# A long-convolution and rational-feed-forward kernel: narrower tiles, and a filter network fed by feature

## The chip, the cores and the metric

The kernel runs on one core of a Trainium2 chip. It has five engines with instruction queues of their own: TensorE (PE in the profile, with its weight loads as PEld), VectorE (DVE), ScalarE (ACT), GpSimd (POOL) and SyncE (SP), which here only issues transfers. The metric is device time of one execution in microseconds. The kernel before takes 2253.34 us, the median of three runs (2252.31 to 2254.02).

## The reference

```python
def _attn_ref(x, v, pos_emb, w1, w2):            # B, S, D = 2, 12480, 128; pos_emb is S x 64
    h_mlp = np.maximum(pos_emb @ w1, 0.0) @ w2
    h_filt = h_mlp * np.exp(-0.01 * np.arange(S))[:, None]
    Uf = np.fft.rfft(x * v, n=2 * S, axis=1)
    Hf = np.fft.rfft(h_filt, n=2 * S, axis=0)
    y = np.fft.irfft(Uf * Hf[None], n=2 * S, axis=1)[:, :S]
    return x * y

def _moe_ref(x, w_in, w_out, a, b):              # x: 24960 x 128, w_in: 128 x 2048
    h = x @ w_in
    P = a[0] + a[1] * h + a[2] * h**2 + a[3] * h**3
    Q = 1.0 + np.abs(b[0]) * np.abs(h) + np.abs(b[1]) * h**2
    return (P / (Q + 1e-06)) @ w_out
```

The result of the first function, seen as 24960 rows, is the input of the second. A long filter is made by a small network from `pos_emb` (the filter network), weighted by a decaying window, and convolved with x·v through a Fourier transform. Then comes a feed-forward layer with a quotient of two polynomials as its nonlinearity.

## The kernel before

**Positions.** A position is written as n = m·128 + residue (`N2` = 128, `H2` = 64). There are 12480 = 97·128 + 64 positions, so a residue below 64 has 98 of them (`M` = 98 rows m) and a residue from 64 up has 97. Of the window only the first 82 rows are used (`MF`).

**Stage one** (batch 0 and the filter) begins with the filter network in 16 blocks of `NP` = 4 pairs of residues, one from the upper half and its mirror from the lower half. `load_pos` fetches `pos_emb` for a block with four transfers on SP's queue, rows m on the partitions (L276). `hf_w` multiplies it by the window with two VectorE instructions of 82 x 256 elements (L480, L486), one block ahead. `hf_t` turns the four pairs by four transposes on TensorE (L500) and copies the result on ScalarE (L503), so that the two times 64 features lie on the partitions. `hf_1` is the product with w1 and the relu (L507, L509), `hf_2` the eight passes of the product with w2 (L515) and four copies (L521). Blocks are pipelined: iteration i runs `hf_t(i)`, `hf_1(i - 1)`, `hf_2(i - 2)`.

Into the same iterations other work is laid. From iteration 5 on each one advances `weights_gen`, which turns a tile of 256 columns of w_in from 64-bit to 32-bit numbers with integer work on VectorE (L330 to L339, L346) and two steps on GpSimd (L341, L455); step k runs in iteration k + 5 and issues the load of tile k + 2 (`raw`, L317). In iterations 0 to 7 a part of x·v is multiplied on GpSimd (L245), and the next parts of x and v are loaded (`xq`, `vq`, L237 and L238). All these loads stand in SP's queue in the order of the code. Each engine takes its instructions in order.

Behind the blocks 32 channel groups go through the transforms. The first of VectorE's work there is L563 (`tb`, 128 x 720), which multiplies by twiddle factors.

**Stage two** is the feed-forward layer: 52 tiles of five residues (or four, at the end of a half), 26 per batch, each in four steps of four blocks of 128 of the 2048 features, 208 steps. All tiles have 98 positions per residue, 490 columns (392 for four residues), whether the last position exists or not. Tiles with p0 below 64 (numbers 0 to 12 and 26 to 38) hold the residues from 64 up. A step computes h with three products (L870 to L872), abs of h (`q`: L880 on halves, or L887 and L893), square of h (`v`, L904), L914 on VectorE, the square of q (L932, L937 on ScalarE, or L942 and L943 on GpSimd for one of the four rows), ln (L948), exp (L953), L959 and L964 on VectorE, L969 and L975 on GpSimd and the product with w_out (L987). A half is two rows of a tile's width (2 x 490 = 980 elements per partition), a whole four. The order in which the steps are issued comes from two strings, `FIRST` for steps 0 to 94 and `REST` for the others; they differ in which engine gets which part of a step. Beside the steps, batch 1's transforms and the next tile's input (`attn_a`, `attn_b`) are laid into slots. `store` copies a finished tile (L998, L1001) and writes it with transfers on SP's queue (L1009). Since the rows of the output are 128 positions apart and pieces may not cross 128 partitions, a tile takes seven or eight of these.

Of the kernel before, what the change touches and what calls it, by code (L numbers as in the profile page):

```python
# [9 lines left out]
F32 = mybir.dt.float32  # L10
# [8 lines left out]
FO = 64  # L19
DFF = 2048  # L20
N2 = 128
M = 98
# [39 lines left out]


def constants():
    t = np.arange(N2)
# [29 lines left out]
    win[:S] = WINDOW  # L95
    win = win.reshape(M, N2)[:96]
    return {
# [12 lines left out]
@with_exitstack  # L110
def build(ctx: ExitStack, tc, x, x_q, v_q, pos_emb, w1, w2, w_in, w_out, moe_a, moe_b,
          f1_d, tw_d, twh_d, dft_d, dfth_d, idfth_d, g_d, win_d, ident_d, out):
# [144 lines left out]
    with ExitStack() as st:  # L257
# [3 lines left out]
        flat = [sp.tile([128, CG * 2 * K1], F32, tag=t, name=t + "0", bufs=2) for t in ("ta", "ta", "tb")]  # L261
        win, bdw1, bdw2 = flat[0][0:96, 0:N2], flat[1][:, 0:128], flat[2][:, 0:2 * D]
        twh = sp.tile([N2, 2, 2 * K1], F32, name="twh")
# [3 lines left out]

        NPL = 4
        pos_t = {}

        def load_pos(p0):
            t = sp.tile([M, 2 * NPL, FO], F32, tag="wa", name="pos", bufs=3)
            for o, t0 in ((0, H2 + p0), (NPL, H2 - p0 - NPL)):
                if MF < M:
                    for r0, r1 in ((0, MF // 16 * 16), (MF // 16 * 16, MF)):
                        nc.sync.dma_start(out=t[r0:r1, o:o + NPL], in_=rows(pos_emb, r0, r1 - r0, t0, NPL, 0, FO))  # L276
                else:
                    load_rows(t[:, o:o + NPL], pos_emb, t0, NPL, 0, FO, True)
            pos_t[p0] = t
# [192 lines left out]

        nb = H2 // NP
        W = NP * MF
        pT, rT = {}, {}

        def hf_w(p0):
            t = pos_t[p0]
            pw = pos_t[p0] = sp.tile([MF, NPL, 2, FO], F32, tag="wb", name="pw", bufs=2)
            nc.vector.tensor_tensor(out=pw[:, :, 0], in0=t[0:MF, 0:NPL],  # L480
                                    in1=win[0:MF, H2 + p0:H2 + p0 + NPL].unsqueeze(2).to_broadcast([MF, NPL, FO]), op=ALU.mult)

            a, w = t[0:MF, 2 * NPL - 1], win[0:MF, H2 - 1 - p0:H2 - p0]
            a = bass.AP(a.tensor, a.offset, [list(a.ap[0]), [-FO, NPL], [1, FO]])
            w = bass.AP(w.tensor, w.offset, [list(w.ap[0]), [-1, NPL], [0, FO]])
            nc.vector.tensor_tensor(out=pw[:, :, 1], in0=a, in1=w, op=ALU.mult)  # L486

        def hf_t(i):
            p0 = i * NP
            b0 = p0 // NPL * NPL  # L490
            if p0 == b0:
                if b0 + 3 * NPL < H2:
                    load_pos(b0 + 3 * NPL)
                if b0 + NPL < H2:
                    hf_w(b0 + NPL)
            pt = pos_t[b0]
            ps = cvs()
# [24 lines left out]

        hf_w(0)
        load_pos(2 * NPL)
        sg = scalars()
# [120 lines left out]
    def second_part(short):  # L646
# [138 lines left out]
        def residue(p0, n):  # L785


            return H2 + p0 if p0 < H2 else N2 - p0 - n

        def load_xg(j):  # L790
            if j >= len(tiles):
                return
            b, p0, n = tiles[j]
            xt = mp.tile([M, NPT, D], F32, tag="xt", name="xt", bufs=2)
            load_rows(xt[:, 0:n], xb[b], residue(p0, n), n, 0, D, True)
            gt = mp.tile([K1, NPT, 2, M], F32, tag="gt", name="gt", bufs=2)
            nc.sync.dma_start(out=gt[:, 0:n], in_=g_d[:, p0:p0 + n])
            xg[j] = (xt, gt)
# [28 lines left out]
        def attn_b(j):  # L827
            n = tiles[j][2]
            w = n * M
            take_up()  # L830
            t = an.pop(j)

            def fill(cv):
                for i in range(n):
                    nc.tensor.transpose(out=cv[:, 0, i * M:(i + 1) * M], in_=t[:, i, :], identity=ident[0:M, 0:M])
# [17 lines left out]
        def width(s):  # L853
            return tiles[steps[s][0]][2] * M

# [134 lines left out]
        def store(j):  # L990
            b, p0, n = tiles[j]
            n0 = residue(p0, n)
            w = n * M
            t = mp.tile([128, 4, D], F32, tag="ot", name="ot", bufs=2)
            a = acc.pop(j)
            nq = (w + 127) // 128
            full = w // 128
            nc.vector.tensor_copy(out=t[:, 0:full, :], in_=a[:, 0:full, :])  # L998
            if full < nq:
                k = w - full * 128  # L1000
                nc.vector.tensor_copy(out=t[0:k, full, :], in_=a[0:k, full, :])  # L1001
            ob = out[b * S:(b + 1) * S, :]
# [73 lines left out]


def by_quarter(x):
# [3 lines left out]
    return a.transpose(0, 4, 2, 1, 5, 3)  # L1082


# [21 lines left out]
```

## Time and profile before

| | us |
|---|---|
| median of three runs | 2253.34 |
| the profiled execution | 2255.12 |
| its span | 2253.2 |
| TensorE busy | 2023.2 (90%) |
| VectorE busy | 2073.7 (92%) |
| ScalarE busy | 1941.2 (86%) |
| GpSimd busy | 2021.5 (90%) |

The span is what the profiler's records cover. The busy shares are means over stages that differ: in the first fortieths of the span ScalarE and GpSimd are about half busy, and the transfers are densest there; in the second half all four engines are over 80%. So what a single stage waits for is read from a view of that stage (busy times by stretch, the timeline, the chain of waits), and the groups by shape give the duration of one instruction. In a timeline row the two numbers are the start and the duration; a bracket tells when the instruction's input was ready and what released it.

### The profile page before, as it was taken

Reading aid. Unit: us, or ns where it says so; the run is one execution under the profiler, and the core shown is the slowest. Engines: PE = TensorE matmul, PEld = TensorE weight load, DVE = VectorE, ACT = ScalarE, POOL = GpSimd, SP = SyncE. Lnnn points to the kernel's source line nnn. Section 1 sums busy time; section 2 is a strip of 40 time slices with the busy share of each in tenths; the row PEclk is TensorE's granted clock in tenths of the full one; section 3 lists DMA queues with packets and bytes.
Section 4 is the critical chain, followed back from the end, with each engine's and each line's share of the span. In section 5 each row is a group of like instructions: output and inputs, shape, how many; then the busy total and the mean of one; then the engine's idle time right before and its main releaser. Section 6 shows DMA issues by size and latency. Waiting matters only on the chain.

```text
span 2253.2 us, 35705 instructions
## 1 busy us (share of the span) xinstructions
PE 2023.2 (90%) x13344; PEld 1758.5 (78%) x13344; DVE 2073.7 (92%) x2374; ACT 1941.2 (86%) x1971; POOL 2021.5 (90%) x1605
## 2 busy tenths in 40 slices
PE   6899987899999999999999889888888898888887
PEld 4678775788888888888888777777777777777775
DVE  6899995899998998999999789999999999999996
ACT  5422224999999998999999899999999999999996
POOL 5488765999999999999999789999999999999997
PEclk9999998999999999999999999999999999999999
DMA  5344415433143233223222212212112111221100
GB/s 159 107 142 143 130 62 146 106 94 81 36 117 80 51 87 83 70 60 76 58 62 52 49 33 46 48 34 46 31 36 49 38 40 33 48 48 33 36 10 11
DMA packets 169487, 150.31 MB, mean 67 GB/s; under 512 B 91622, under 2 KB 138984, under 8 KB 166424
## 3 DMA queue, kind: packets, MB, share of 16 engines
q1 hardware_dynamic: 162280, 124.17, 22.5%
q10 hardware_dynamic: 7024, 23.76, 3.2%
q8 instruction: 107, 1.75, 0.3%
q14 instruction: 76, 0.62, 0.1%
HBM read 99.72 MB, written 48.17 MB: 66 GB/s over the span
## 4 chain that ended last, share of the span: by engine, by line
ACT 41%; POOL 22%; PE 22%; DVE 7%; issue 5%; DMA 2%; SPq 1%; POOLq 0%; DVEq 0%; ACTq 0%
POOL v L975 10%; ACT v L904 10%; ACT l L948 9%; ACT r L953 9%; PE acc L987 5%; POOL v L969 4%; ACT q L880 4%; ACT q L937 4%; ACT q L932 3%; PE cs L155 3%; PE cs L582 2%; POOL q L943 2%; PE cv L816 2%; PE h L870 1%; PE h L872 1%
## 5 line engine op out<-in xcount | busy, mean ns | idle before, releaser
L975 POOL TENSOR_TENSOR v<-v,q 128x980 f32<-128x980 f32 (+1 forms) x416 | 940.6, 2262 | 52.0 <-DVE q L964 48.7
L987 PE MATMUL acc<-wout,v 128*128 128x128 f32 (+2 forms) x6656 | 846.2, 280 | 112.4 <-POOL v L975 108.0
L987 PEld LDWEIGHTS acc<-wout,v 128*128 128x128 f32 (+2 forms) x6656 | 776.6, 187 | 191.5 <-POOL v L975 165.8
L959 DVE SCALAR_TENSOR_TENSOR q<-q,sc,r 128x980 f32<-128x980 f32 (+1 forms) x416 | 504.6, 1213 | 36.3 <-ACT r L953 34.9
L914 DVE SCALAR_TENSOR_TENSOR v<-v,sc,h 128x980 f32<-128x980 f32 (+1 forms) x416 | 504.7, 1213 | 35.4 <-ACT q L880 30.4
L964 DVE SCALAR_TENSOR_TENSOR q<-q,r 128x980 f32<-128x980 f32 (+1 forms) x416 | 482.0, 1159 | 13.5
L904 ACT ACTIVATE v<-h,sc 128x980 f32<-128x980 f32 (+1 forms) x416 | 438.1, 1082 | 30.9 <-PE h L872 29.4
L953 ACT ACTIVATE r<-l 128x980 f32<-128x980 f32 (+1 forms) x416 | 416.8, 1002 | 9.8 <-DVE q L964 8.9
L969 POOL TENSOR_SCALAR v<-v,sc 128x980 f32<-128x980 f32 (+3 forms) x321 | 422.3, 1316 | 0.0
L948 ACT ACTIVATE l<-q,sc 128x1960 f32<-128x1960 f32 (+1 forms) x208 | 401.1, 1928 | 0.7 <-POOL q L943 0.5
L870 PE MATMUL h<-ahi,win_l 128*128 128x490 f32 (+1 forms) x832 | 360.9, 434 | 28.6 <-DVE v L914 26.6
L871 PE MATMUL h<-alo,win_h 128*128 128x490 f32 (+1 forms) x832 | 319.6, 384 | 0.0
L872 PE MATMUL h<-ahi,win_h 128*128 128x490 f32 (+1 forms) x832 | 317.6, 382 | 0.0
L880 ACT ACTIVATE q<-h 128x980 f32<-128x980 f32 (+1 forms) x303 | 302.5, 998 | 8.9 <-PE h L872 8.8
L870 PEld LDWEIGHTS h<-ahi,win_l 128*128 128x128 f32 x832 | 158.6, 191 | 60.5 <-DVE v L914 38.4
L932 ACT ACTIVATE q<-q,sc 128x1960 f32<-128x1960 f32 (+1 forms) x95 | 185.9, 1957 | 0.0
L872 PEld LDWEIGHTS h<-ahi,win_h 128*128 128x128 f32 x832 | 158.0, 190 | 26.0
L937 ACT ACTIVATE q<-q,sc 128x1470 f32<-128x1470 f32 (+1 forms) x113 | 170.6, 1510 | 0.0
L871 PEld LDWEIGHTS h<-alo,win_h 128*128 128x128 f32 x832 | 159.2, 191 | 13.5 <-DVE alo L841 0.4
L816 PE MATMUL cv<-yc,gt 90*98 90x128 f32 x1004 | 127.9, 274 | 2.2 <-DVE an L822 1.0
L816 PEld LDWEIGHTS cv<-yc,gt 90*98 90x98 f32 x1004 | 118.3, 165 | 14.1 <-DVE an L822 7.5
L943 POOL TENSOR_TENSOR q<-q 128x490 f32<-128x490 f32 (+1 forms) x113 | 111.4, 986 | 9.4
(113 smaller groups left out, 2623.5 us busy)
## 6 DMA issues: line engine op xcount, KB each, us to landing
yc<-y_d SPq DMA_DIRECT2D x23, 900.0 KB
gt<-in_g_dram SPq DMA_DIRECT2D x48, 344.5 KB
xq<-in_x_q_dram SPq DMA_DIRECT2D x64, 196.0 KB
vq<-in_v_q_dram SPq DMA_DIRECT2D x64, 196.0 KB
h_d<-hg ACTq DMA_DIRECT2D x32, 360.0 KB
y_d<-ys ACTq DMA_DIRECT2D x16, 720.0 KB
hg<-h_d SPq DMA_DIRECT2D x64, 180.0 KB
y_d<-ys SPq DMA_DIRECT2D x16, 720.0 KB
```

The lines of the kernel that those rows point to most:

```text
L870: nc.tensor.matmul(out=t[:, k, 0:w], lhsT=wl, rhs=hi[:, 0:w], start=True, stop=False)
L871: nc.tensor.matmul(out=t[:, k, 0:w], lhsT=wh, rhs=lo[:, 0:w], start=False, stop=False)
L872: nc.tensor.matmul(out=t[:, k, 0:w], lhsT=wh, rhs=hi[:, 0:w], start=False, stop=True)
L904: nc.scalar.activation(out=v, in_=st_h[s, i], func=AF.Square, bias=col("s"))
L914: stt(out=v, in0=v, scalar=col("k"), in1=h, op0=ALU.add, op1=ALU.mult)
L948: nc.scalar.activation(out=part(st_l, s, i), in_=part(st_q, s, i), func=AF.Ln, **({"bias": col("ka")} if short else {}))
L953: nc.scalar.activation(out=t[:, :, 0:w], in_=halves(st_l[s], i, w), func=AF.Exp, scale=-1.0)
L959: nc.vector.scalar_tensor_tensor(out=q, in0=q, scalar=col("ka") if short else 0.0, in1=st_r[s, i], op0=ALU.add, op1=ALU.mult)
L964: nc.vector.scalar_tensor_tensor(out=q, in0=q, scalar=2.0, in1=st_r.pop((s, i)), op0=ALU.subtract, op1=ALU.mult)
L969: nc.gpsimd.tensor_scalar(out=v, in0=v, scalar1=col("p0" if short else "a0"), scalar2=1.0, op0=ALU.add, op1=ALU.mult)
L975: nc.gpsimd.tensor_tensor(out=v, in0=v, in1=halves(st_q[s], i, w), op=ALU.mult)
L987: nc.tensor.matmul(out=acc[j][0:k, q // 128, :], lhsT=g[:, i, q:q + k], rhs=wout[:, f, :], start=(f == 0 and q == 0), stop=(f == NF - 1), ...
```

## The change

Three things are changed.

Tiles of residues from 64 up are 97 positions wide: 485 columns (388 for four residues). The products (L858 to L860 in the new numbering) take an even number of columns, so one more than 485 is computed and not used; all later work has exactly the tile's width.

The output has another order in memory, residue by residue, and is put back into the reference's order on the host (`by_position`). A tile is then one contiguous piece, written by two transfers.

The filter network gets `pos_emb` in an order made on the host (`by_feature`), two times 64 features on the partitions and 4 x 82 positions along a row, so that a block is one transfer of 128 x 328 elements. The window is laid out the same way, as two rows of 328 per block, and each row is read for 64 partitions by a second transfer (`win`). Both are issued three blocks ahead. One VectorE instruction of 328 elements (L485) multiplies them. The transposes, the ScalarE copy and the multiply one block ahead are gone.

```diff
+def by_pair(a):
+    a = np.moveaxis(a[:MF], (0, 1), (-1, -2))
+    a = np.stack([a[..., H2:, :], a[..., H2 - 1::-1, :]])
+    return np.moveaxis(a.reshape(a.shape[:-2] + (H2 // NP, NP * MF)), -2, 0)
...
-    win = win.reshape(M, N2)[:96]
+    win = by_pair(win.reshape(M, N2))
...
-        def load_pos(p0):
-            t = sp.tile([M, 2 * NPL, FO], F32, tag="wa", name="pos", bufs=3)
-            for o, t0 in ((0, H2 + p0), (NPL, H2 - p0 - NPL)):
...
-                    for r0, r1 in ((0, MF // 16 * 16), (MF // 16 * 16, MF)):
-                        nc.sync.dma_start(out=t[r0:r1, o:o + NPL], in_=rows(pos_emb, r0, r1 - r0, t0, NPL, 0, FO))
...
+        def load_pos(i):
+            t = sp.tile([128, W], F32, tag="wa", name="pos", bufs=3)
+            w = sp.tile([128, W], F32, tag="wn", name="win", bufs=3)
+            nc.sync.dma_start(out=t, in_=pos_q[i])
+            nc.sync.dma_start(out=w, in_=win_d[i].unsqueeze(1).to_broadcast([2, FO, W]))
+            pos_t[i] = (t, w)
 
         load_pos(0)
-        nc.sync.dma_start(out=win, in_=win_d)
         nc.sync.dma_start(out=ident, in_=ident_d)
-        load_pos(NPL)
+        load_pos(1)
+        load_pos(2)
...
-        def hf_w(p0):
...
         def hf_t(i):
...
-            for p in range(NP):
-                k = p0 - b0 + p
-                nc.tensor.transpose(out=ps[:, 0, p * MF:(p + 1) * MF], in_=pt[:, k].rearrange("m t c -> m (t c)"),
-                                    identity=ident[0:MF, 0:MF])
-            pT[i] = ctile(sp, "zh", 2, CG).rearrange("p r c k -> p (r c k)")[:, 0:W]
-            nc.scalar.activation(out=pT[i], in_=ps[:, 0, 0:W], func=AF.Identity)
+            t, w = pos_t.pop(i)
+            if i + 3 < nb:
+                load_pos(i + 3)
+            pT[i] = sp.tile([128, W], F32, tag="wb", name="pw", bufs=2)
+            nc.vector.tensor_tensor(out=pT[i], in0=t, in1=w, op=ALU.mult)
...
+        def count(j):
+            return M if tiles[j][1] >= H2 else M - 1
...
         def attn_b(j):
             n = tiles[j][2]
-            w = n * M
+            k1 = count(j)
+            w = n * k1 + n * k1 % 2
...
         def width(s):
-            return tiles[steps[s][0]][2] * M
+            j = steps[s][0]
+            return tiles[j][2] * count(j)
...
         def mm1(s, i):
             j, c = steps[s]
             w = width(s)
+            w += w % 2
...
-            st_h[s, i] = t[:, :, 0:w]
+            st_h[s, i] = t[:, :, 0:width(s)]
...
         def store(j):
...
-            w = n * M
+            w = n * count(j)
...
-            p = 0
-            while p < w:
-                i, m = divmod(p, M)
-                k = min(M - m, 128 - p % 128)
-                mm = min(k, (M if n0 + i < H2 else M - 1) - m)
-                if mm > 0:
-                    nc.sync.dma_start(out=ob[bass.DynSlice(m * N2 + n0 + i, mm, step=N2), :],
-                                      in_=t[p % 128:p % 128 + mm, p // 128, :])
-                p += k
+            r0 = b * S + n0 * M - max(0, n0 - H2)
+            ob = out[r0:r0 + w, :]
+            nc.sync.dma_start(out=ob[0:full * 128, :].rearrange("(q p) c -> p q c", p=128), in_=t[:, 0:full, :])
+            nc.sync.dma_start(out=ob[full * 128:w, :], in_=t[0:k, full, :])
```

Three places show how instructions move. The names are those of the program's tiles; the numbers behind them are partitions by elements.

The first is SP's queue at the start of the program, the loads of the first filter blocks. Before:

```order
L276 DMA pos<-in_pos_emb_dram 80x256
L276 DMA pos<-in_pos_emb_dram 2x256
L276 DMA pos<-in_pos_emb_dram 80x256
L276 DMA pos<-in_pos_emb_dram 2x256
L282 DMA ta_85<-in_win_dram 96x128
L283 DMA ident<-in_ident_dram 128x128
```

Now:

```order
L282 DMA pos<-in_pos_q_dram 128x328
L283 DMA win<-in_win_dram 128x1x328
L287 DMA ident<-in_ident_dram 128x128
L282 DMA pos<-in_pos_q_dram 128x328
L283 DMA win<-in_win_dram 128x1x328
L282 DMA pos<-in_pos_q_dram 128x328
L283 DMA win<-in_win_dram 128x1x328
L244 DMA xq<-in_x_q_dram 98x512
L245 DMA vq<-in_v_q_dram 98x512
```

The one load of the whole window at the start (into `ta_85`) is gone, and a `win` load stands behind every `pos` load, 16 in all; three blocks are asked for before the first `xq` and `vq`.

The second is VectorE in one filter block, from the L339 of one weight step (`f` is the converted tile, `i_` its integer parts, `pw` the windowed positions) on. Before:

```order
L339 SCALAR_TENSOR_TENSOR f<-i_539,i_538 128x256
L480 TENSOR_TENSOR pw<-pos,ta_85 82x4x64
L486 TENSOR_TENSOR pw<-pos,ta_85 82x4x64
L346 SCALAR_TENSOR_TENSOR f<-i_540,f 128x256
L330 TENSOR_SCALAR i_584<-raw 128x256
```

Now:

```order
L344 SCALAR_TENSOR_TENSOR f<-i_451,i_450 128x256
L485 TENSOR_TENSOR pw<-pos,win 128x328
L351 SCALAR_TENSOR_TENSOR f<-i_452,f 128x256
L335 TENSOR_SCALAR i_487<-raw 128x256
```

Two multiplies between L339 and L346 have become one, which now stands one block later than before (block i's multiply in iteration i, not i - 1) and reads `win` in place of the window that was loaded once. Behind the last multiply of the blocks there were four weight steps' L339 before L563, and there are three of the same line, L344, before the same work, now L543.

The third is SP's queue at the store of one tile of five residues. Before:

```order
L1009 DMA out_dram<-ot 97x128
L1009 DMA out_dram<-ot 30x128
L1009 DMA out_dram<-ot 67x128
L1009 DMA out_dram<-ot 60x128
L1009 DMA out_dram<-ot 37x128
L1009 DMA out_dram<-ot 90x128
L1009 DMA out_dram<-ot 7x128
L1009 DMA out_dram<-ot 97x128
```

Now:

```order
L990 DMA out_dram<-ot 128x3x128
L991 DMA out_dram<-ot 101x128
```

Eight transfers have become two; the first writes the tile's three full columns of 128 rows, the second the rest.

## Rows read from the trace of the kernel before

**Rows 1.** Busy us by stretch: PE, PEld, DVE, ACT, POOL; clock; DMA; GB/s.
```profile
971.20:1200.20 229.00, 220.10 (x1566) 203.30 (x1566) 216.04 (x217) 228.30 (x211) 214.35 (x181) 1.00 0.26 63
...
1483.20:1750.90 267.70, 235.79 (x1604) 204.06 (x1605) 262.61 (x273) 267.63 (x258) 265.03 (x193) 1.00 0.20 41
```

**Rows 2.** Chain of waits from 1600 to 1640 us, shares by line.
```profile
by line: POOL v L975 56.5%; POOL v L969 26.5%; POOL q L943 12.5%; POOL q L942 6.5%; issue 0.7%; POOLq L975 0.2%
```

**Rows 3.** Groups by line and shape: count | busy us, mean ns | idle before.
```profile
L975 POOL TENSOR_TENSOR v<-v,q 128x980 f32<-128x980 f32 x384 | 880.8, 2295 | 45.0 <-DVE q L964 41.7 <-ACT q L932 3.1
...
L904 ACT ACTIVATE v<-h,sc 128x980 f32<-128x980 f32 x384 | 409.2, 1096 | 26.0 <-PE h L872 24.5
...
L969 POOL TENSOR_SCALAR v<-v,sc 128x980 f32<-128x980 f32 x202 | 219.4, 1086 | 0.0
...
L975 POOL TENSOR_TENSOR v<-v,q 128x784 f32<-128x784 f32 x32 | 59.8, 1868 | 7.0 <-DVE q L964 7.0
...
L904 ACT ACTIVATE v<-h,sc 128x784 f32<-128x784 f32 x32 | 29.2, 925 | 5.0 <-PE h L872 5.0
...
L969 POOL TENSOR_SCALAR v<-v,sc 128x784 f32<-128x784 f32 x24 | 22.2, 923 | 0.0
```

**Rows 4.** Timeline of a filter block: start us, us, engine, line, operation.
```profile
54.05 0.42 DVE L339 SCALAR_TENSOR_TENSOR f<-i,i 128x256 f32<-128x256 int32 x1 [0.63 <-POOL win_l L455]
...
54.56 0.84 POOL L341 TENSOR_TENSOR f<-f,i 128x256 f32<-128x256 f32 x1 [0.54 <-DVE f L339]
...
54.73 0.94 DVE L486 TENSOR_TENSOR pw<-pos,ta 82x256 f32<-82x256 f32 x1
...
57.99 0.42 DVE L339 SCALAR_TENSOR_TENSOR f<-i,i 128x256 f32<-128x256 int32 x1 [0.63 <-POOL win_l L455]
```

**Rows 5.** Timeline, end of the filter blocks, VectorE.
```profile
66.53 0.94 DVE L486 TENSOR_TENSOR pw<-pos,ta 82x256 f32<-82x256 f32 x1
...
69.79 0.43 DVE L339 SCALAR_TENSOR_TENSOR f<-i,i 128x256 f32<-128x256 int32 x1 [0.63 <-POOL win_l L455]
...
71.05 0.42 DVE L346 SCALAR_TENSOR_TENSOR f<-i,f 128x256 f32<-128x256 int32 x1 [0.84 <-POOL f L341]
...
72.93 0.43 DVE L339 SCALAR_TENSOR_TENSOR f<-i,i 128x256 f32<-128x256 int32 x1
...
79.55 0.90 DVE L563 TENSOR_TENSOR tb<-cs,twh 128x720 f32<-128x720 f32 x1
```

**Rows 6.** Timeline of SP after the last tile.
```profile
2245.68 3.44 SPq L1009 DMA_DIRECT2D out_dram<-ot  x7
```

**Rows 7.** Transfers from 432.2 to 442.8 us in 40 slices; issues.
```profile
DMA  9897955754220001001400520000000045699968
GB/s 216 315 310 216 226 207 194 277 185 154 69 81 19 21 21 27 21 21 35 118 19 23 139 76 23 23 21 21 21 21 21 21 75 108 230 354 344 356 193 209
...
out_dram<-ot SPq DMA_DIRECT2D x2, 48.5 KB
out_dram<-ot SPq DMA_DIRECT2D x1, 45.0 KB
out_dram<-ot SPq DMA_DIRECT2D x1, 33.5 KB
...
out_dram<-ot SPq DMA_DIRECT2D x1, 18.5 KB
```

**Rows 8.** Timeline of the start, SP and VectorE.
```profile
0.73 1.43 SPq L276 DMA_DIRECT2D pos<-in_pos_emb_dram  x4
...
2.21 0.32 SPq L282 DMA_DIRECT2D ta<-in_win_dram  x1
...
4.23 0.42 DVE L480 TENSOR_TENSOR pw<-pos,ta 82x256 f32<-82x256 f32 x1 [4.23 <-DMA ta<-in_win_dram]
```

**Rows 9.** Timeline, two products of the filter network on TensorE.
```profile
27.59 3.62 PE L515 MATMUL cs<-tb,zu 128*82 128x256 f32 x8
...
70.80 1.89 PE L515 MATMUL cs<-tb,zu 128*82 128x256 f32 x8
```

More of the change, by code (lines that the diff above doesn't have):

```diff
@@ L110, in build @@
 @with_exitstack
-def build(ctx: ExitStack, tc, x, x_q, v_q, pos_emb, w1, w2, w_in, w_out, moe_a, moe_b,
+def build(ctx: ExitStack, tc, x, x_q, v_q, pos_q, w1, w2, w_in, w_out, moe_a, moe_b,
           f1_d, tw_d, twh_d, dft_d, dfth_d, idfth_d, g_d, win_d, ident_d, out):
@@ L261, in build @@
         flat = [sp.tile([128, CG * 2 * K1], F32, tag=t, name=t + "0", bufs=2) for t in ("ta", "ta", "tb")]
-        win, bdw1, bdw2 = flat[0][0:96, 0:N2], flat[1][:, 0:128], flat[2][:, 0:2 * D]
+        bdw1, bdw2 = flat[1][:, 0:128], flat[2][:, 0:2 * D]
         twh = sp.tile([N2, 2, 2 * K1], F32, name="twh")
@@ L266, in build @@
         hf = [sp.tile([M, UQ, N2], F32, tag="hu", name=f"hf{q}", bufs=6) for q in range(D // UQ)]
-        NPL = 4
+        W = NP * MF
+        nb = H2 // NP
         pos_t = {}
-        def load_pos(p0):
-            t = sp.tile([M, 2 * NPL, FO], F32, tag="wa", name="pos", bufs=3)
-            for o, t0 in ((0, H2 + p0), (NPL, H2 - p0 - NPL)):
-                if MF < M:
-                    for r0, r1 in ((0, MF // 16 * 16), (MF // 16 * 16, MF)):
-                        nc.sync.dma_start(out=t[r0:r1, o:o + NPL], in_=rows(pos_emb, r0, r1 - r0, t0, NPL, 0, FO))
-                else:
-                    load_rows(t[:, o:o + NPL], pos_emb, t0, NPL, 0, FO, True)
-            pos_t[p0] = t
+        def load_pos(i):
[4 more added lines that the diff above has]
+            pos_t[i] = (t, w)
         load_pos(0)
-        nc.sync.dma_start(out=win, in_=win_d)
         nc.sync.dma_start(out=ident, in_=ident_d)
-        load_pos(NPL)
+        load_pos(1)
+        load_pos(2)
         nc.gpsimd.memset(bdw1, 0.0)
@@ L521, in hf_2 @@
                 nc.scalar.activation(out=o, in_=a, func=AF.Identity)
-        hf_w(0)
-        load_pos(2 * NPL)
         sg = scalars()
@@ L834, in fill @@
                 for i in range(n):
-                    nc.tensor.transpose(out=cv[:, 0, i * M:(i + 1) * M], in_=t[:, i, :], identity=ident[0:M, 0:M])
+                    k = min(M, w - i * k1) if i == n - 1 else k1
+                    nc.tensor.transpose(out=cv[:, 0, i * k1:i * k1 + k], in_=t[0:k, i, :], identity=ident[0:k, 0:k])
             def take(cv):
@@ L992, in store @@
             n0 = residue(p0, n)
-            w = n * M
+            w = n * count(j)
             t = mp.tile([128, 4, D], F32, tag="ot", name="ot", bufs=2)
             a = acc.pop(j)
-            nq = (w + 127) // 128
             full = w // 128
+            k = w - full * 128
             nc.vector.tensor_copy(out=t[:, 0:full, :], in_=a[:, 0:full, :])
[L999 to L1002, printed above, removed]
-            p = 0
-            while p < w:
-                i, m = divmod(p, M)
-                k = min(M - m, 128 - p % 128)
-                mm = min(k, (M if n0 + i < H2 else M - 1) - m)
-                if mm > 0:
-                    nc.sync.dma_start(out=ob[bass.DynSlice(m * N2 + n0 + i, mm, step=N2), :],
-                                      in_=t[p % 128:p % 128 + mm, p // 128, :])
-                p += k
+            nc.vector.tensor_copy(out=t[0:k, full, :], in_=a[0:k, full, :])
+            r0 = b * S + n0 * M - max(0, n0 - H2)
+            ob = out[r0:r0 + w, :]
+            nc.sync.dma_start(out=ob[0:full * 128, :].rearrange("(q p) c -> p q c", p=128), in_=t[:, 0:full, :])
+            nc.sync.dma_start(out=ob[full * 128:w, :], in_=t[0:k, full, :])
         at = []
@@ L1075, with by_position @@
 _OUTS = [((B * S, D), "float32")]
+def by_position(a):
+    a = a.reshape(B, S, D)
+    r = np.empty_like(a)
+    o = 0
+    for n in range(N2):
+        k = M if n < H2 else M - 1
+        r[:, n::N2] = a[:, o:o + k]
+        o += k
+    return r.reshape(B * S, D)
 def by_quarter(x):
@@ L1082, in by_quarter, with by_feature @@
     return a.transpose(0, 4, 2, 1, 5, 3)
+def by_feature(x):
+    a = np.zeros((M * N2, FO), np.float32)
+    a[:S] = x
+    return by_pair(a.reshape(M, N2, FO)).reshape(H2 // NP, 2 * FO, NP * MF)
 def kernel(**inputs):
@@ L1091 @@
     feeds = [("x", inputs["x"]), ("x_q", by_quarter(inputs["x"])), ("v_q", by_quarter(inputs["v"]))]
-    feeds += [(n, inputs[n]) for n in _INS[2:]] + list(constants().items())
+    feeds += [("pos_q", by_feature(inputs["pos_emb"]))] + [(n, inputs[n]) for n in _INS[3:]] + list(constants().items())
     for name, a in feeds:
@@ L1104 @@
     r = _run(nc, [arrays], core_ids=[0])
-    return r.results[0]["out_0_dram"]
+    return by_position(np.asarray(r.results[0]["out_0_dram"]))
```

19 lines of the change are left out of this document (removed).

## Prediction

> **What bounds the kernel now.** I read the program in its three stages, since the busy shares of the whole span mix stages with different limits. For the matmul stage I took the busy times in two steady stretches [rows 1]. Between 971.20 and 1200.20 us (the first order of steps, in use up to step 94) ScalarE is busy for 228.30 of 229.00 us: it sets the pace. Between 1483.20 and 1750.90 (the second order) ScalarE and GpSimd are both full, 267.63 and 265.03 of 267.70, and the chain of waits runs over GpSimd alone, 56.5% of it in L975 [rows 2]. The groups by shape [rows 3] show the same lines at 980 and at 784 elements, so what one element costs is a difference of two rows.
>
> For the filter stage (blocks 0 to 15) I read the timeline. Blocks from number 8 on come every 3.94 us (L339 at 54.05 and at 57.99), and what lies between is a ring of VectorE and GpSimd work: L339, GpSimd L341, the second window multiply L486, which starts at 54.73 and ends 0.27 us after L341 does (55.67 against 55.40), and then the weight step's conversions [rows 4]. TensorE, ScalarE and the loads follow it. The first DFT work of VectorE, L563, starts at 79.55, right behind three weight steps that follow the last window multiply's block [rows 5]. All later work of stage one queues behind it on VectorE, which hardly idles there: a shift of this L563 shifts the end one for one.
>
> **The change, part by part.**
>
> *Tiles of 97 positions.* 26 of the 52 tiles (those with p0 below 64, numbers 0 to 12 and 26 to 38) get 485 columns in place of 490, or 388 in place of 392; that is 104 of 208 steps, 52 under each order. ScalarE under the first order handles per step six halves of 980 (L880, L904, L953 twice each) and two wholes of 1960 (L932, L948), 9800 elements, of which 100 go. One element costs (1096 - 925) / 196 = 0.87 ns [rows 3]: 87 ns a step, 48 steps of 100 elements and 4 of 80, 4.5 us. GpSimd under the second order has per step L975 twice ((2295 - 1868) / 196 = 2.18 ns), L969 twice ((1086 - 923) / 196 = 0.83 ns) and L942 and L943 on one row of 490, for which I take 0.83 and 2.18 as well: 43.6 + 16.6 + 15 = 75 ns a step, 3.8 us; ScalarE, equally full, saves about as much. The 784 rows are already two pieces of 392 at a pitch of 490, so the two-piece pattern that 485 makes of 980 is priced in them. TensorE saves four columns per product and next to nothing in L987, but has idle time in both stretches [rows 1]. Sum -8.3 us; I take -8.0, between -5 (the next ring takes over part of it) and -8.5. An odd row length stands in no row: see the rivals.
>
> *Stores.* 8 or 7 strided transfers per tile become two. Inside the kernel nothing waits for them. At the end the seven issues take 3.44 us, 0.49 us each [rows 6]; two take about 1.0. The last one lands that much earlier: -2.4 us (-1.5 to -2.7).
>
> *Filter blocks: what goes.* Per block two multiplies of 256 elements become one of 328, four transposes and one ScalarE copy go. The ring loses L486's 0.27 us and gains 72 elements of about 1 ns: -0.2 us a block, some -2 us over ten blocks. The copy of ScalarE and the transposes were beside the ring. At the start a little more may go, since the moe_a load no longer queues behind a copy: 0 to -3. If nothing else stood in the way, the stage would end 3.5 us earlier (2 to 5).
>
> *Filter blocks: what is added.* Each block now loads `win`, 128 rows of 1312 bytes, 167,936 bytes, from two rows in memory that are read 64 times each. The trace of before has no such transfer, so I go by how transfers spread. In the first store eight pieces were issued; the view of transfers shows stretches at 19 to 27 GB/s and bumps far above [rows 7]. The flat stretches are the pieces of 97, 67, 37 and 97 rows (48.5, 33.5, 18.5 and 48.5 KB), counts without a divisor: they run on one engine, and on the same one, since four of them in flight never add up to more than about 21. The piece of 90 rows (45.0 KB) is a bump. So a transfer takes a number of engines that divides the count it starts with, and a small number means always the same engines. `win` starts with 2 on the memory side and 128 in SBUF; only 1 and 2 divide both. I take two engines: 83,968 bytes each. An engine's rate lies between 21 GB/s (the flat stretch, 512-byte rows) and 25 (the peak of 356 GB/s over 16 engines at a busy share of 9 tenths [rows 7]); near the second for rows above 1 KB, I take 23. One `win` then takes 3.65 us against 0.46 if it were spread over 16.
>
> The Trainium skill (DMA: Bandwidth & Descriptors, section "Why a DMA increments its semaphore by 16 and not by 1") states it as a rule: the number of engines is the largest up to 16 that divides the slowest dimension larger than one of both sides, and they are the lowest-numbered ones. By that rule `win` has two engines; by a reading of the SBUF side alone it would have 16. The trace agrees on the prime counts; no run here shows a transfer whose two sides differ.
>
> Three blocks of lead hide a latency, not a full queue. Per block one of these two engines gets 84.0 KB of `win`, 10.5 of `pos`, up to block 9 twice 14.3 of `xq` and `vq` (98 rows, 14 engines) and from block 5 on 16.4 of `raw`. That is 5 to 6 us, more than the 3.94 of the ring. So the queue sets the pace. Up to the last `win` it holds 16 x 84.0 + 16 x 10.5 + 20 x 14.3 + 9 x 16.4 KB = 1.946 MB (thousands of bytes): 84.6 us. A first transfer issued at 0.73 starts to flow at about 1.7, an estimate from the `win` load of before (issued at 2.21, its reader starts at 4.23 [rows 8]); the last `win` has landed at 86.3. Behind it in the same queue stand f1, twh, dfth and a `raw` tile, 41 KB, 1.8 us; this `raw` is what the weight step of iteration 14 waits for (step k loads the tile of step k + 2), and VectorE takes its work in order. At 88.1 it starts; conversions and L339 need about 1.5 us (L346 at 71.05 to L339 at 72.93, less L346 itself [rows 5]), so L339 of that step starts at 89.7. From there before had 9.76 us to L563 (69.79 to 79.55); the last multiply now lies in between, mostly in a gap: +0.25. L563 at 99.7 against 79.55: **+20.2 us**. At 25 GB/s the queue takes 77.8 us (+13), at 21 it takes 92.7 (+28). The gains of the paragraph before are swallowed, since VectorE waits. Queued behind these waits are the weight steps on VectorE, with them L341 and the window products on GpSimd, and the `xq` loads behind the `pos` loads on SP's queue; none of them is ahead of the end of the queue.
>
> **Sum.** +20.2 - 8.0 - 2.4 = +9.8 us. The profiled execution took 2255.12 us (span 2253.2), 1.8 above the median of 2253.34; 2255.12 + 9.8 = 2264.9 for such an execution, 2263 for the median.
>
> **Rivals.**
> *Spread loads.* If `win` runs on 16 engines (or on two that change from transfer to transfer), an engine has 66 KB per block, 2.9 us, less than the ring's 3.94; nothing waits. Then -3.5 - 8.0 - 2.4 = -13.9: 2239.5 us. For it: 128 rows in SBUF are enough for 16 engines. Against it: the prime counts of [rows 7], and the fixed engine. It decides wherever one block's load of the busiest engine stays under 3.94 us, which is 91 KB at 23 GB/s.
> *Odd rows.* Two engines as forecast, and no gain from 97 positions, because 485-element rows run slower on ScalarE or GpSimd: +17.8, 2271 us. Against it: per-element costs from 784 to 980 are straight on both engines.
> *Slow clock.* With TensorE idle for several us before the last blocks, its products can run at half speed: the eight of L515 took 3.62 us after such an idle time and 1.89 otherwise [rows 9]. The last three groups lie partly on the way to L563; +2 to +5 us on top of the forecast. I keep it in the range.
>
> **How the numbers follow.** Forecast with its ends (2256 to 2273): 0.70; spread loads (2237 to 2243): 0.22; odd rows or no gain from the widths (2268 to 2276): 0.08. 0.2% (4.5 us) is about what a measurement can tell from no change. Of the forecast's 0.70, 0.06 lies within it (the rate at its upper end with the full gain elsewhere); slower is 0.64 + 0.06, faster 0.22 and a little. The range must reach into the second case: 2240 to 2273; the likeliest one's own is 2256 to 2273.
>
> **What would show it.** Of the profile after: in the first 90 us the transfer view lies flat at 40 to 50 GB/s for long stretches with a busy share of about two sixteenths; the window multiply of VectorE waits on `win` in nearly every block, blocks come every 4.7 to 6 us, and the first L563 (now L543) starts near 100 us. A step of a narrower tile gets about 87 ns shorter where ScalarE sets the pace and 75 ns where GpSimd does; the other 104 steps stay as they are. The last issue of the store to the end shrinks by some 2.4 us. I am wrong if `win` lands within about 2.5 us of its issue, or if the first DFT work of VectorE starts before 85 us.

## The result, and the profile after

The changed kernel takes 2269.68 us (median of six runs, 2266.99 to 2271.67) against 2253.68 for the kernel before in the same comparison: a ratio of 1.0067, 95% interval 1.0055 to 1.0078. The profiled execution took 2270.16 us (span 2268.1), 15.0 more than that of before. The forecast was 2263, slower, with 2240 to 2273 as its range; the sign and the mechanism came true, and the two largest terms had other sizes. The wide range reached into a rival; the forecast's own, 2256 to 2273, held too, by 3.3 us.

The end of the filter blocks is where the time went. This is VectorE's timeline after (start, duration, engine, line; in brackets how long it had waited, and for what), to be read beside [rows 5].

```profile
47.84 0.50 DVE L485 TENSOR_TENSOR pw<-pos,win 128x328 f32<-128x328 f32 x1 [2.16 <-DMA win<-in_win_dram]
...
60.06 0.29 DVE L335 TENSOR_SCALAR i<-raw 128x256 int32<-128x256 int32 x1 [1.70 <-DMA raw<-in_moe_w_in_dram]
...
66.48 0.30 DVE L335 TENSOR_SCALAR i<-raw 128x256 int32<-128x256 int32 x1 [2.50 <-DMA raw<-in_moe_w_in_dram]
...
91.68 0.30 DVE L335 TENSOR_SCALAR i<-raw 128x256 int32<-128x256 int32 x1 [1.74 <-DMA raw<-in_moe_w_out_dram]
...
93.57 0.49 DVE L485 TENSOR_TENSOR pw<-pos,win 128x328 f32<-128x328 f32 x1
...
103.17 0.90 DVE L543 TENSOR_TENSOR tb<-cs,twh 128x720 f32<-128x720 f32 x1
```

The first twiddle multiply starts at 103.17 in place of 79.55. From 60 us on blocks come 4.5 to 6.4 us apart (L335 from 60.06 to 66.48), and VectorE waits for a load in each. In blocks 4 to 7 the load is `win` (the multiply at 47.84 is block 7's); from block 8 on it is the `raw` tile queued behind a `win`. The transfers from 31 to 46 us (40 slices, busy tenths and GB/s) show what holds them, beside [rows 7]:

```profile
DMA  9621111111256999631111112769986321011111
GB/s 287 168 61 53 59 49 49 49 49 49 71 120 256 340 332 275 139 109 67 49 45 49 45 49 65 125 228 333 347 270 135 133 74 71 31 38 38 49 49 49
```

For stretches of 2 to 3 us one tenth of the engines' time is busy, two engines of 16, and they move 49 GB/s. The chain of waits up to 104 us says the same in shares, and the view of SP's waits shows that loads are also held before they are issued: `vq` loads (L245) and `win` loads (L283) wait on SP for a `win` to land (us in all, times, longest).

```profile
by line: DMA win<-in_win_dram 37.5%; DMA raw<-in_moe_w_in_dram 19.6%; DMA raw<-in_moe_w_out_dram 7.0%; DMA sc<-in_moe_a_dram 5.0%; issue 4.3%; DVE sc L369 3.3%; PE cs L497 3.2%; SPq L519 3.0%; PE cs L162 2.6%; ACT hf L503 2.4%; DMA vq<-in_v
```

```profile
SPq L245 <- DMA win<-in_win_dram: 7.0, 4, 2.9
SPq L283 <- DMA win<-in_win_dram: 5.6, 5, 1.5
...
SPq L283 <- DMA ident<-in_ident_dram: 3.0, 1, 3.0
```

The groups by shape after, to be read beside [rows 3], give the price of a narrower instruction directly:

```profile
L963 POOL TENSOR_TENSOR v<-v,q 128x980 f32<-128x980 f32 x192 | 440.4, 2294 | 30.8 <-DVE q L952 28.6 <-ACT q L920 2.1
L963 POOL TENSOR_TENSOR v<-v,q 128x970 f32<-128x970 f32 x192 | 437.9, 2283 | 15.1 <-DVE q L952 13.9 <-ACT q L920 1.0
...
L892 ACT ACTIVATE v<-h,sc 128x980 f32<-128x980 f32 x192 | 205.0, 1097 | 11.8 <-PE h L860 10.8
L892 ACT ACTIVATE v<-h,sc 128x970 f32<-128x970 f32 x192 | 203.2, 1084 | 14.4 <-PE h L860 14.1
...
L957 POOL TENSOR_SCALAR v<-v,sc 128x980 f32<-128x980 f32 x106 | 115.2, 1087 | 0.0
L957 POOL TENSOR_SCALAR v<-v,sc 128x970 f32<-128x970 f32 x96 | 104.5, 1089 | 0.0
```

Ten elements fewer take 11 ns off GpSimd's multiply, 13 off ScalarE's square and nothing off GpSimd's add-and-scale. Busy times by stretch (columns as in [rows 1]) of the 48 steps of the first twelve narrower tiles, from GpSimd's multiply in step 0 to the one in step 48, and of the 52 steps of the thirteen in batch 1 (steps 104 to 156). Before:

```profile
387.20:850.80 463.60, 435.18 (x3054) 399.43 (x3054) 429.17 (x430) 455.24 (x420) 448.15 (x369) 0.99 0.33 83
...
1382.00:1815.90 433.90, 384.89 (x2611) 331.10 (x2610) 421.95 (x443) 429.75 (x418) 426.02 (x313) 1.00 0.19 40
```

After:

```profile
408.10:870.00 461.90, 433.97 (x3059) 398.72 (x3057) 426.40 (x430) 451.91 (x420) 445.41 (x368) 0.99 0.33 83
...
1401.30:1832.65 431.35, 382.78 (x2610) 330.57 (x2610) 418.80 (x443) 427.11 (x417) 423.33 (x313) 1.00 0.18 40
```

The first stretch is 1.7 us shorter, 35 ns a step; the second 2.55 us, 49 ns. The 46 steps up to the switch of the orders, 42 of them of wider tiles, last as long as before (436.90 us from step 48 to 94 before, 437.00 after). The store at the end, beside [rows 6]:

```profile
2262.71 0.39 SPq L990 DMA_DIRECT2D out_dram<-ot  x1
2263.19 0.60 SPq L991 DMA_DIRECT2D out_dram<-ot  x1
```

Two issues in 1.08 us in place of 3.44. From the last GpSimd multiply's start to the span's end it is 10.9 us after (2257.20 to 2268.1) and 12.5 before (2240.73 to 2253.2).

Together, as shifts of the changed kernel against before at the same piece of work: +23.6 at the first twiddle multiply, +20.9 at GpSimd's multiply of step 0, +19.2 at step 52, +19.2 at step 104, +16.7 at step 156, +16.5 at the last multiply, +14.9 at the end.

### The profile page after: what moved, and what is told of

Same layout as the page of the kernel before. It is cut to its first block, busy times and chain, and to the rows that moved or that the text cites. A ratio compares the mean times of both kernels' runs of the same rounds, so it can differ in the third digit from the quotient of the medians.

```text
span 2268.1 us, 35100 instructions
## 1 busy us (share of the span) xinstructions
PE 2026.7 (89%) x13280; PEld 1759.9 (78%) x13280; DVE 2064.7 (91%) x2358; ACT 1931.6 (85%) x1955; POOL 2000.1 (88%) x1605
## 4 chain that ended last, share of the span: by engine, by line
ACT 41%; POOL 23%; PE 21%; DVE 6%; issue 4%; DMA 4%; SPq 0%; POOLq 0%; ACTq 0%; DVEq 0%
POOL v L963 11%; ACT v L892 10%; ACT l L936 9%; ACT r L941 8%; PE acc L975 6%; POOL v L957 5%; ACT q L868 4%; ACT q L920 4%; ACT q L925 3%; PE cs L162 3%; POOL q L931 2%; PE cv L800 2%; PE cs L562 2%; DMA win<-in_win_dram 2%; PE h L858 1%
## 5 line engine op out<-in xcount | busy, mean ns | idle before, releaser
L963 POOL TENSOR_TENSOR v<-v,q 128x970 f32<-128x970 f32 (+3 forms) x416 | 937.6, 2255 | 52.5 <-DVE q L952 49.2
L975 PE MATMUL acc<-wout,v 128*128 128x128 f32 (+4 forms) x6656 | 846.7, 280 | 115.1 <-POOL v L963 110.5
L975 PEld LDWEIGHTS acc<-wout,v 128*128 128x128 f32 (+4 forms) x6656 | 776.0, 186 | 195.2 <-POOL v L963 168.9
L947 DVE SCALAR_TENSOR_TENSOR q<-q,sc,r 128x970 f32<-128x970 f32 (+3 forms) x416 | 502.6, 1208 | 35.4 <-ACT r L941 34.1
L902 DVE SCALAR_TENSOR_TENSOR v<-v,sc,h 128x970 f32<-128x970 f32 (+3 forms) x416 | 502.8, 1209 | 34.6 <-ACT q L868 27.5
L952 DVE SCALAR_TENSOR_TENSOR q<-q,r 128x970 f32<-128x970 f32 (+3 forms) x416 | 480.1, 1154 | 13.4
L892 ACT ACTIVATE v<-h,sc 128x970 f32<-128x970 f32 (+3 forms) x416 | 437.0, 1077 | 31.1 <-PE h L860 29.9
L941 ACT ACTIVATE r<-l 128x970 f32<-128x970 f32 (+3 forms) x416 | 414.6, 997 | 9.5 <-DVE q L952 8.9
L957 POOL TENSOR_SCALAR v<-v,sc 128x980 f32<-128x980 f32 (+6 forms) x321 | 422.2, 1315 | 0.1
L936 ACT ACTIVATE l<-q,sc 128x1940 f32<-128x1940 f32 (+3 forms) x208 | 399.1, 1919 | 0.8 <-POOL q L931 0.5
L858 PE MATMUL h<-ahi,win_l 128*128 128x486 f32 (+3 forms) x832 | 360.4, 433 | 25.4 <-DVE v L902 23.6
L860 PE MATMUL h<-ahi,win_h 128*128 128x486 f32 (+3 forms) x832 | 317.5, 382 | 0.0
L858 PEld LDWEIGHTS h<-ahi,win_l 128*128 128x128 f32 x832 | 158.6, 191 | 55.9 <-DVE v L902 32.3
L860 PEld LDWEIGHTS h<-ahi,win_h 128*128 128x128 f32 x832 | 158.2, 190 | 25.7
```

The source lines that it names most:

```text
L858: nc.tensor.matmul(out=t[:, k, 0:w], lhsT=wl, rhs=hi[:, 0:w], start=True, stop=False)
L892: nc.scalar.activation(out=v, in_=st_h[s, i], func=AF.Square, bias=col("s"))
L902: stt(out=v, in0=v, scalar=col("k"), in1=h, op0=ALU.add, op1=ALU.mult)
L936: nc.scalar.activation(out=part(st_l, s, i), in_=part(st_q, s, i), func=AF.Ln, **({"bias": col("ka")} if short else {}))
L941: nc.scalar.activation(out=t[:, :, 0:w], in_=halves(st_l[s], i, w), func=AF.Exp, scale=-1.0)
L947: nc.vector.scalar_tensor_tensor(out=q, in0=q, scalar=col("ka") if short else 0.0, in1=st_r[s, i], op0=ALU.add, op1=ALU.mult)
```

## The experiments

Theory A, the prediction's: the `win` load runs on two engines because its source begins with a count of two, and the queue of these two engines sets the pace. Rival B: reading one row of memory 64 times is slow however many engines do it. Rival C: a lead of three blocks is too short for a transfer's latency. Four kernels came first; **lead2**, for rival C, was added last.

**full**: the window lies in memory once for each of the 128 partitions.

```diff
-            nc.sync.dma_start(out=w, in_=win_d[i].unsqueeze(1).to_broadcast([2, FO, W]))
+            nc.sync.dma_start(out=w, in_=win_d[i])      # win repeated 64 times on the host
```

> The changed kernel, but the window factors lie in memory once per partition, so a block's win load is 128 rows of 1312 bytes read from 128 rows; bytes and number of transfers are the same. Theory A (a transfer uses a number of engines that divides the first count of both sides; two rows in memory mean two engines): 16 engines, an engine gets 66 KB a block, about 3.0 us at the 22 GB/s that the two engines moved in the changed kernel, less than the 3.94 us of the ring of before; no wait on win, the first twiddle multiply of VectorE near 76 us instead of 103.17, time 2241 us (2238 to 2246). Rival B (reading one row of memory 64 times is what is slow, on however many engines): also fast here, 2241. If the time stays above 2260, both are wrong.

Measured: 2245.55 us (2243.9 to 2245.76), ratio to before 0.9958 (0.9944 to 0.9971). First twiddle multiply at 78.26; the transfers from 31 to 46 us have no flat stretch left:

```profile
DMA  8998996211369997889628489796998510639988
GB/s 306 300 301 237 313 315 229 82 49 16 66 268 344 360 197 191 236 276 379 230 104 131 104 317 387 241 150 130 262 363 328 203 60 11 71 76 344 360 299 147
```

**dose2**: nothing is read twice, but the 128 rows lie as two groups of 64 with one row of padding between.

```diff
-            nc.sync.dma_start(out=w, in_=win_d[i])
+            nc.sync.dma_start(out=w, in_=win_d[i, :, 0:64])    # win_d: block, 2 groups, 64 + 1 rows, 328
```

> As the run full, but the 128 rows lie in memory as two groups of 64 with a gap of one row between them; nothing is read twice. Theory A: the first count is 2 again, so two engines, a busy share of 2 of 16 in long stretches, first twiddle multiply near 103 us, time 2270 us (2266 to 2273). Rival B: nothing is re-read, so as fast as full, 2241 us.

Measured: 2270.82 us (2267.82 to 2271.97), ratio 1.0068 (1.0054 to 1.0082), the changed kernel's time. The flat stretches are back, from 31 to 46 us:

```profile
DMA  6211111157789852111111238997531101111136
GB/s 224 70 52 49 49 52 49 52 101 150 296 293 335 229 161 95 49 49 49 49 49 45 64 112 334 328 301 212 168 140 49 64 31 38 42 49 51 50 79 166
```

This takes rival B away: the same rate, 49 GB/s, without a single row read twice.

**dose4**: four groups of 32.

```diff
-            nc.sync.dma_start(out=w, in_=win_d[i, :, 0:64])    # win_d: block, 2 groups, 64 + 1 rows, 328
+            nc.sync.dma_start(out=w, in_=win_d[i, :, 0:32])    # win_d: block, 4 groups, 32 + 1 rows, 328
```

> As dose2, but four groups of 32 rows. Theory A: four engines with 42.0 KB of win each per block; up to the last win their queue holds 1.27 MB in place of 1.95, 58 us at 22 GB/s, less than the blocks take by themselves; only in blocks 5 to 9, with 97 KB on the busiest engines (4.4 us), can it fall behind by 1 to 2 us. First twiddle multiply at 76 to 79 us, time 2241 to 2245, within 3 us of full. Rival B: as full. Were the time rather proportional to the queue's length from the start, it would lie half way, near 2255.

Measured: 2249.95 us (2248.57 to 2252.95), ratio 0.9981 (0.9972 to 0.999); first twiddle multiply at 82.58. Its flat stretches have two tenths busy and twice the rate, here in a view of 24 to 34 us:

```profile
DMA  3789974222222222103677175589777998696959
GB/s 147 301 330 298 292 213 80 63 89 105 100 103 104 98 98 106 49 33 37 84 257 268 37 85 109 184 295 289 216 216 257 333 291 191 174 221 188 207 198 289
```

About 100 GB/s against 49: the number of engines follows the count. The packet records of the traces say the same: between 1.7 and 92 us exactly two packets are in flight for 27.8 us in the changed kernel and for 0.9 us here, exactly four for 2.2 and 10.5 us. The kernel is 4.4 us slower than full and its first twiddle multiply 4.3 us later; both lie beyond what was expected (within 3 us, and 76 to 79). It is still far from half way to dose2: once the queue is shorter than the blocks take by themselves, most of its length costs nothing.

**spread_two**: each row still read 64 times, in two transfers of 64 partitions.

```diff
-            nc.sync.dma_start(out=w, in_=win_d[i].unsqueeze(1).to_broadcast([2, FO, W]))
+            for s in range(2):
+                nc.sync.dma_start(out=w[s * FO:(s + 1) * FO], in_=win_d[i, s:s + 1].to_broadcast([FO, W]))
```

> The changed kernel with each win load cut into two transfers, one for each row in memory, read 64 times each as before. Theory A: both sides now begin with 64, so 16 engines each; no wait on win, time as full plus at most 2 us for 16 more issues on SP's queue: 2241 to 2244. Rival B: each row is still read 64 times, so the time stays near 2270.

Measured: 2243.35 us (2242.31 to 2244.79), ratio 0.995 (0.9937 to 0.9964); first twiddle multiply at 76.82. Repeated reads cost nothing that can be seen. Of all kernels run it is the fastest by median, and it beats both the kernel before and the changed one. That it beats full by 2.2 us is not put down to the edit (see the last section).

**lead2**: the changed kernel with loads two blocks ahead.

```diff
-        load_pos(2)
...
-            if i + 3 < nb:
-                load_pos(i + 3)
+            if i + 2 < nb:
+                load_pos(i + 2)
```

> The changed kernel with its loads two blocks ahead in place of three. Theory A (the two engines' queue is never empty and its length in bytes sets the end): the bytes are the same, a block takes 5 to 6 us and a win load about 3.4, so two blocks still cover it: first twiddle multiply at 101 to 106 us, time 2267 to 2274, the same as the changed kernel. Rival C (a lead of three blocks is too short for the latency of these loads): a third less lead makes every block wait longer, by a third of the blocks' excess over 3.9 us or more: first multiply at 112 us or later, time 2278 or more.

Measured: 2269.8 us (2267.82 to 2270.64), ratio 1.0071 (1.0057 to 1.0085); first twiddle multiply at 103.02. Rival C falls: a block of lead less changes nothing. The packet records show why: from 1.7 to 92 us fewer than two packets are in flight for 0.3 us in all, in the changed kernel and in lead2 alike, against 21 us in full, so the queue is hardly ever empty. A longer lead was not tried.

Three more kernels undo one of the other parts each, from full, so that the queue does not cover them; a fourth changes the odd row length.

**wide**: work on 490 columns again, residues still packed 97 apart. One more transpose in each narrower tile fills the last columns, and the tile's two conversions on VectorE run over them as well.

```diff
...
         def width(s):
-            j = steps[s][0]
-            return tiles[j][2] * count(j)
+            return tiles[steps[s][0]][2] * M
...
```

> The run full with the narrower tiles undone for all work behind the tile's input: residues are still packed 97 apart, but products, polynomial and quotient run over 490 (392) columns, the last of which are filled with other values and never stored. It prices the widths alone against full (2245.55). By the prediction's term (87 ns a step under the first order, 75 under the second, 52 steps each): +8.0, 2253.5 us. By the trace of the changed kernel (33 ns and 48 ns a step, what GpSimd's instructions got shorter): +4.3 to +5, 2250 us, and the steps of the first half of each batch last 33 and 48 ns longer than in full, the others the same.

Measured: 2248.76 us (2245.91 to 2250.5), ratio 0.9972 (0.9963 to 0.9981), 3.2 above full. A loss of 8.0 would be a ratio of 0.9993 and lies outside the interval. The 3.2 may lack some 2 us: in the profiles the ten steps around the switch of the two orders take 92.4 us in wide and 94.3 in full (see the last section). By stretches (the same steps as above) full has 462.10 and 431.40 us, wide:

```profile
384.70:849.60 464.90, 440.01 (x3069) 402.36 (x3067) 429.23 (x430) 455.01 (x420) 448.14 (x369) 0.99 0.33 82
...
1378.90:1813.20 434.30, 387.65 (x2623) 333.23 (x2624) 422.07 (x443) 430.15 (x418) 426.09 (x313) 1.00 0.18 40
```

That is 2.8 and 2.9 us, 58 and 56 ns a step: more than the 35 and 49 between before and after, and still below 87 and 75. Wide does a little more than before in these steps (TensorE is busy 440.01 us in the first stretch, 435.18 before), so the price of the widths lies between the two pairs.

**pieces**: the strided stores and the reference's order of the output.

```diff
-            r0 = b * S + n0 * M - max(0, n0 - H2)
-            ob = out[r0:r0 + w, :]
-            nc.sync.dma_start(out=ob[0:full * 128, :].rearrange("(q p) c -> p q c", p=128), in_=t[:, 0:full, :])
-            nc.sync.dma_start(out=ob[full * 128:w, :], in_=t[0:k, full, :])
+            ob = out[b * S:(b + 1) * S, :]
+            k1 = count(j)
+            p = 0
+            while p < w:
+                i, m = divmod(p, k1)
+                k = min(k1 - m, 128 - p % 128)
+                nc.sync.dma_start(out=ob[bass.DynSlice(m * N2 + n0 + i, k, step=N2), :],
+                                  in_=t[p % 128:p % 128 + k, p // 128, :])
+                p += k
```

> The run full with the stores undone: the output in the reference's order again, seven or eight strided transfers per tile. By the prediction's term the end is 2.4 us later, 2248 us; by the trace of the changed kernel 2.0, from the last copy of a tile to the end, 2247.6. Rival: the stores also hold back loads that stand behind them on SP's queue in each tile, then the steps in the middle grow as well and it is over 2249.

Measured: 2246.93 us (2242.73 to 2248.25), ratio 0.9964 (0.995 to 0.9977), 1.4 above full with overlapping intervals. In its trace the seven issues of the last tile take 2.93 us and the end lies 12.4 us behind the start of the last GpSimd multiply, against 10.7 in full.

**oldfilter**: the filter network of before, with the new widths and stores.

```diff
-            t, w = pos_t.pop(i)
-            if i + 3 < nb:
-                load_pos(i + 3)
-            pT[i] = sp.tile([128, W], F32, tag="wb", name="pw", bufs=2)
-            nc.vector.tensor_tensor(out=pT[i], in0=t, in1=w, op=ALU.mult)
+            ...      # load_pos, hf_w and hf_t as in the kernel before
```

> The kernel before with the narrower tiles and the two-transfer stores alone; the filter network with its four loads a block, transposes and window multiplies one block ahead is that of before. Prediction's term for what the filter network gains once its loads do not wait: 3.5 us, so 2249. By the trace of full (first twiddle multiply at 78.26 against 79.55): 1.3 us, so 2247. Rival: the gain is on the way only in the profile and the times are equal, 2245.5.

Measured: 2247.75 us (2246.04 to 2251.09), ratio 0.9971 (0.9961 to 0.9982), 2.2 above full, again with overlapping intervals. So the filter network by feature, well loaded, is worth about 2 us by the medians and not told from nothing by the intervals, and the kernel without it is faster than before too. Its profiled execution is the slowest of its eight (2251.09).

**even**: tiles of 485 columns worked on as 486.

```diff
...
-            return tiles[j][2] * count(j)
+            return tiles[j][2] * count(j) // 2 * 2 + tiles[j][2] * count(j) % 2 * 2
...
```

> The run full with an even row: tiles of 485 columns are worked on as 486 (one more column that is computed and not stored). If an odd row length is what took away GpSimd's gain (its add-and-scale took 1089 ns for 2 x 485 elements and 1087 for 2 x 490, but 916 for 2 x 388 and 922 for 2 x 392), that line takes about 1080 ns for 2 x 486, and a step of the second order gets up to 14 ns shorter: -0.5 us, hardly to be seen in the time, but plainly in the line. If the duration goes in jumps of another kind, the line stays at 1087 or so and the time stays at 2245.5.

Measured: 2244.76 us (2242.2 to 2247.79), ratio 0.9962 (0.9949 to 0.9976), no difference from full. The two GpSimd groups at the new width:

```profile
L963 POOL TENSOR_TENSOR v<-v,q 128x972 f32<-128x972 f32 x192 | 438.0, 2284 | 14.2 <-DVE q L952 13.1 <-ACT q L920 1.0
...
L957 POOL TENSOR_SCALAR v<-v,sc 128x972 f32<-128x972 f32 x96 | 103.7, 1080 | 0.0
```

The add-and-scale takes 1080 ns, 7 less than with two elements fewer (1087 in full): on two rows the odd length is what had eaten its gain. On four rows it shows no such effect: 1904 ns at 4 x 485 in full, 1905 at 4 x 486, 1919 at 4 x 490. The multiply with two inputs does not change (2284 against 2281 in full), so its smaller gain per element is not explained by this.

## Why the prediction was right, and where it was off

*Two engines: right.* The changed kernel, dose2, dose4, spread_two and full agree on it; a busy share of two sixteenths and about 49 GB/s had been named beforehand (40 to 50). The rule of the Trainium skill (DMA: Bandwidth & Descriptors, section "Why a DMA increments its semaphore by 16 and not by 1"), the largest number up to 16 that divides the first counts of both sides, is borne out by dose2 and dose4, where the two sides of a transfer differ: 2 and 4 engines, with 128 on the other side.

*The queue sets the pace: right, and 3.5 us too short.* The step that was off is the rate, "I take 23". The queue up to the last `raw` is 1.987 MB (1.946 and 41 KB); flowing from 1.7, an estimate (the first packet of `pos` starts at 1.8 in the packet records), it ended at 91.68, where VectorE's conversion of that tile starts, and not at 88.1: 90.0 us, 22.1 GB/s an engine. Alone the two engines make 24.5 each (half of 49), but beside other traffic a packet takes longer: 1312 bytes take 57 ns on average with fewer than three packets in flight and 79 ns with ten or more. The queue lives in both. The sum also left out `ident` and the loads on ScalarE's queue, by an estimate 15 KB an engine (64 KB and 0.17 MB over 16 engines), 0.7 of the 3.5 us. Behind it the sum held: L344 1.54 us after the conversion began (1.5 forecast), L543 at 9.95 us after that (10.01 forecast).

*What VectorE waits for: half right.* The window multiply waited for `win` four times, not in nearly every block. In the later blocks the conversion of a `raw` tile came first in VectorE's order and took the wait upon itself. It makes no difference to the time, but whoever had looked for `win` alone among VectorE's waits would have found 6.8 us of some 22.

*Narrower tiles: right in sign, half to seven tenths in size.* -8.0 was forecast; the two stretches gave -1.7 and -2.55 between before and after, and 2.8 and 2.9 between full and wide. Under the first order ScalarE's price per element was sound for the instructions: its five lines together are 4.5 us shorter in full than before over these 48 steps, where 4.2 was priced. The step that failed is the view, which engine sets the pace. The stretch of [rows 1] that shows ScalarE alone as full holds wider tiles, late in the first order; while the narrower tiles run, batch 1's products are still on GpSimd, and of 463.60 us ScalarE is busy 455.24 and GpSimd 448.15. Under the second order the 40 us of [rows 2], with GpSimd alone on the chain, are not the whole stage. The chains over the narrower tiles, first order before, second order before and after:

```profile
by line: ACT v L904 10.3%; POOL v L975 9.5%; ACT l L948 8.7%; ACT q L880 8.0%; ACT r L953 7.8%; PE acc L987 7.4%; ACT q L932 7.1%; issue 5.6%; POOL uq L245 3.5%; POOL v L969 3.3%; PE cv L816 3.3%; PE h L872 2.0%; PE h L870 2.0%; ACT qt L222
...
by line: POOL v L975 26.5%; POOL v L969 12.1%; ACT v L904 10.5%; ACT r L953 9.9%; ACT l L948 9.7%; ACT q L937 7.6%; POOL q L943 5.9%; issue 5.5%; POOL q L942 3.7%; PE acc L987 2.1%; ACT q L887 1.3%; DVE q L959 1.1%; DVE v L914 0.9%; DVE q L
...
by line: ACT v L892 18.8%; ACT l L936 18.2%; ACT r L941 17.9%; ACT q L925 14.0%; issue 8.1%; POOL v L963 4.6%; ACT q L875 4.3%; PE acc L975 3.9%; POOL v L957 1.9%; DVE q L947 1.1%; POOL q L931 1.1%; DVE q L952 1.0%; PE h L858 1.0%; DVE v L9
```

Under the first order the chain runs 42% over ScalarE's five lines and 13% over GpSimd's L975 and L969; under the second it runs 48% over GpSimd's four lines before and over ScalarE for most of it after. So the two share the bound. How a step's saving divides between them is not shown: under the first order GpSimd's two lines lost 1.9 us in full, 40 ns a step, near the 35 that a step lost, but no run makes one of the two engines alone faster. GpSimd's per-element price from 784 to 980 did not hold for ten elements either: 11 ns for 22 on the multiply, 0 for 8 on the add-and-scale. The rival on odd rows thus had a piece of the truth on one line in its two-row form, and even shows it.

*Stores: right, and smaller.* -2.4 was forecast; the end came closer by 1.6 us measured from the last GpSimd multiply's start, and 1.7 us separate pieces from full. One profile does not fit: oldfilter has the two-transfer stores, and its end lies 12.4 us behind that start, as far as before. There the two issues end at 2243.36 and the span 5.8 us later, against 4.3 in the changed kernel; no run tells why.

*The gain of the filter network if nothing waited:* 3.5 us was forecast (2 to 5). The first twiddle multiply of full is 1.3 us earlier than that of before and those of the kernels with the same filter network 2.1 to 2.8; the times of oldfilter and full differ by 2.2. It cost the forecast nothing here, since the waits covered it, but together with the size of the widths it makes the rival "spread loads" too fast: 2239.5 was named, and full takes 2245.55.

*Slow clock:* TensorE's eight products took 3.40 us in one of the late blocks, where the granted clock from 84.70 to 88.10 was 0.50, the lower level of 1.2 GHz; TensorE had been idle for 1.96 us just before, up to 83.83. At the upper level (from 88.20 on) the next eight took 1.89. VectorE did not wait for them: L543 follows right behind the weight steps. No cost.

*Left open:* between the first twiddle multiply and step 0 the changed kernel gained 2.7 us. The other kernels' profiles lie between a gain of 2.7 and a loss of 2.7 in the same stretch, oldfilter at the latter, and no run here tells why. This gain stands in no term of the forecast; without it the time would have come near 2272, close to the range's upper end.

## What to carry to other kernels

Before a load is called hidden, count the engines that it can use. Two rows that are each read for 64 partitions make a transfer that begins with a count of two on one side; here it ran on two engines, and everything else on these engines queued with it. The cure costs one line: let both sides begin with a count that 16 divides, as with one transfer per source row. And price a narrower instruction in the stretch where it runs, from the chain of the whole stretch: the engine that bounds the same steps elsewhere may share the bound there.

## What the runs showed of the hardware

GpSimd's add-and-scale of two rows takes 1087 to 1089 ns with 485 elements a row, 1080 with 486 and 1087 with 490; of four rows 1904 to 1908, 1905 and 1919 to 1920. Two engines move 49 GB/s and four about 100 with rows of 1312 bytes when the others rest; a row of 1312 bytes takes 57 ns on average with fewer than three packets in flight and 79 ns with ten or more (changed kernel). The ten steps around the switch of the two orders (from GpSimd's multiply of step 94 to that of step 104) took one of two lengths in the profiles, 94.2 to 94.4 us in before, after, full, dose2, dose4, pieces and even, and 92.4 to 92.6 in spread_two, lead2, wide and oldfilter, whatever was changed; differences of 2 us between two of these kernels are therefore not put down to their edits.
